# One block's scores and state sums moved behind the products of the block before, in the same four PSUM banks, and counted semaphore events put into TensorE's stream

## The chip, the cores and the metric

The kernel runs on one core of a Trainium2 chip. The metric is the device time of one execution in microseconds; the time before is the median of three runs. Profiles come from one more execution, which the hardware profiler records. TensorE is called PE, VectorE DVE, ScalarE ACT, GpSimd POOL and SyncE SP.

## The reference, cut to what matters

```python
# x: (4, 8, 768, 32), a: (4, 8, 768), B and C: (4, 8, 768, 16); chunks of 32 tokens
L = np.exp(cum[:, :, :, None] - cum[:, :, None, :]) * causal   # cum: running sum of log a
CB = np.einsum('bhin,bhjn->bhij', Cc, Bc)
y_intra = np.einsum('bhij,bhjd->bhid', CB * L, xc)
y_inter = np.einsum('bhin,bhnd->bhid', Cc, state) * np.exp(cum)[:, :, :, None]
Bx = np.einsum('bhjn,bhjd->bhjnd', Bc, xc) * np.exp(cum[:, :, -1:] - cum)[..., None, None]
state = np.exp(np.sum(la, axis=-1))[:, :, None, None] * state + np.sum(Bx, axis=2)
...
h = y @ w_in                                   # y as (3072, 256), w_in (256, 2048)
g = np.where(h > 0.0, h, np.exp(np.minimum(h, 0.0)) - 1.0)
out = g @ w_out                                # w_out (2048, 256)
```

A scan over tokens, with a state of 16 x 32 per head, gives y; a feed-forward layer with ELU follows.

## The kernel before, in words

The 3072 tokens are cut into twelve blocks of 256 tokens (8 heads each), three to a batch. The kernel scans in chunks of 64 tokens; u and v number a block's halves of 128 tokens and the halves of these. The blocks are numbered in the order of the work, so that neighbours belong to different batches. The whole order of the work is written out by hand, on every engine: an engine runs its instructions in the order in which the program gives them, and waits where an operand or a buffer isn't ready. PSUM has eight banks of 2 KB: seven rotate in one pool (p_a, tag "a"), one belongs to p_o. A tile takes the next bank of the rotation, and its first writer waits for the last reader of what was there before. The waits are put in by the framework, tile by tile.

The steps of block n, with the lines that the profile shows:

- Loads on SP's queue: `load_bc` (B and C, L140, in halves u), `load_x` (xr, L156), `spread_exp` (ec, the spread exponentials of the running sums, L404).
- `scaled` (L416 to 422): B times the decay factors, on the engine that is named (tile sc).
- `turn` (L436): four PE transposes (L442), of B into ps_tb and of C into ps_tc; ACT copies ps_tb to bt (L447); DVE makes ctm, C masked by heads (L450).
- `turn_exp` (L454): DVE multiplies ps_tc by ec into cts (L458). It is the last reader of ps_tc.
- `decay` (L553, L561): ACT takes exponentials of L, the decays of token pairs; POOL masks them (L566).
- `scores` (L572, L582): 32 small PE products from bt and ctm, into four banks ps_g, one for each pair of heads. `weigh` (L588, L591): DVE multiplies one bank by L into M.
- `sums` (L603, L612): 32 small products of sc and x into two banks ps_st. `states` (L619): DVE adds them to the running state (L629), POOL masks each new state into Sx (L634).
- `across` (L645, L660): products of Sx and cts into four banks ps_y. `inside` (L668, L678): products of M and x into the same banks; then six copies to yT (L695), on ACT for blocks 2 and 3.

The feed-forward layer of blocks 0 and 1, and the first half of it for blocks 2 and 3, uses plain float32 products: `l1` (L709, L716; eight products into a bank ps_h), `elu` (ACT L730 and L737, DVE L738) and `l2` (L893). For the second half of w_in's columns of blocks 2 and 3, and for all from block 4 on, two blocks together are done by `l1_words` (L824, L835): three passes over operands split into rounded words, six products for each m, joined by ACT and DVE; the words of y come from DVE, the tile y_both at L818. Behind each of these products for blocks 4 to 9 and m < 9 stands a sem_inc on a spare semaphore that nothing waits for (L838 to L840).

The stretch of the change is the loop over s (L1167 to L1209), which gives one l1 of blocks 0 and 1 for each s from 0 to 11 and lays the scan of block 2 between them: turn(2) at s=5, scores(2) at s=7, states(2) at s=8, across(2) and inside(2) at s=10. The loop over j that follows (L1233 to L1281; eight steps of one l1 of block 2 and one l2 of block 0) lays out block 3: scaled, turn and turn_exp at j=0, scores, sums and weigh at j=1, states at j=2, across and inside at j=3. Meanwhile w_out arrives in pieces that ACT, DVE and POOL round (L205 to L249). The loop j=8 to 15 (L1282 on) gives l1_words(2, j), an l2 of block 1 and the scan of blocks 4 and 5; the loop from L1368 on does the pairs of blocks from 4.

```python
                if 2 < n < 10 and m < 9:
                    for _ in range(1 + (n > 4 and k == 0)):
                        nc.tensor.sem_inc(spare, 1)
```

Of the kernel before, what the change touches and what calls it, by code (L numbers as in the profile page):

```python
# [17 lines left out]
P = 128  # L18
# [15 lines left out]
def kernel(  # L34
# [56 lines left out]
    def psum(shape, name):  # L91
        return p_a.tile(shape, F32, tag="a", name=name)
# [460 lines left out]
    def decay(n, q):  # L553

        decay_of(n, 2 * q)
        decay_of(n, 2 * q + 1)
# [12 lines left out]

    def scores(*ns, pool=p_a, tag="a"):  # L572

        gs = [psum([P, len(ns), 2, 2, Q], "ps_g") for _ in range(3)]
        gs.append(pool.tile([P, len(ns), 2, 2, Q], F32, tag=tag, name="ps_g"))
        for at, n in enumerate(ns):
            s = st[n]
            for u in range(2):
                for v in range(2):
                    for q in range(4):  # L580
                        rows, toks = slice(32 * q, 32 * q + 32), slice(Q * v, Q * v + Q)
                        nc.tensor.matmul(  # L582
                            out=gs[q][toks, at, u], lhsT=s["bt"][rows, u, toks],
                            rhs=s["ctm"][rows, u, :, toks], start=True, stop=True,
                            tile_position=(32 * q, Q * v), skip_group_check=True)
            s["g"], s["M"] = [g[:, at] for g in gs], []
# [13 lines left out]

    whole, most, last = slice(0, 4), slice(0, 3), slice(3, 4)

    def sums(*ns, pool=p_a, tag="a", parts=(None, None)):  # L603

        ps = [psum([P, len(ns), 2, 2 * D], "ps_st"),
              pool.tile([P, len(ns), 2, 2 * D], F32, tag=tag, name="ps_st")]
        for at, n in enumerate(ns):
            s = st[n]
            for u, v in chunks(n, parts[at] or whole):
                toks = slice(Q * v, Q * v + Q)  # L610
                for q in range(4):
                    nc.tensor.matmul(  # L612
                        out=ps[v][32 * q:32 * q + 32, at, u],
                        lhsT=s["sc"][toks, u, 2 * q:2 * q + 2].rearrange("p h n -> p (h n)"),
                        rhs=s["x"][toks, u, 2 * D * q:2 * D * (q + 1)], start=True, stop=True,
                        tile_position=(Q * v, 32 * q), skip_group_check=True)
            s["st"] = [p[:, at] for p in ps]
# [24 lines left out]

        return 2 * D * v if n else 0

    def across(*ns, pool=p_a, tag="a", halves=(0, 1)):  # L645


        y = [None, None]
        for t in halves:
            y[t] = [psum([P, len(ns), 2, Q], "ps_y"), (p_a if t else pool).tile(  # L650
                [P, len(ns), 2, Q], F32, tag="a" if t else tag, name="ps_y")]
        for u in (1, 0):
            for at, n in enumerate(ns):
                for v in range(2):
                    Sx = starts.get((n, u, v))
                    if Sx is None:
                        continue
                    for q in range(2 * halves[0], 2 * halves[-1] + 2):
                        rows, col = slice(32 * q, 32 * q + 32), (64 * q + shift(n, v)) % P
                        nc.tensor.matmul(  # L660
                            out=y[q // 2][v][col:col + 64, at, u],
                            lhsT=Sx[rows].rearrange("p k d -> p (k d)"),
                            rhs=st[n]["cts"][rows, u, Q * v:Q * v + Q],
                            start=(u == 1 and at == 0), stop=False,
                            tile_position=(32 * q, col), skip_group_check=True)
        return y

    def inside(y, *ns, t=None):  # L668
# [27 lines left out]
        if t:  # L696
            for n in ns:
                st.pop(n)


    g_of = {}

# [116 lines left out]
                out=both[:, k], in0=y1[:, k].bitcast(F32), scalar=1.0 - WORD,  # L819
                in1=y[:, k], op0=ALU.mult, op1=ALU.add)  # L820

    spare = tc.alloc_semaphore("spare")

    def l1_words(n, m, ahead=None, ahead_of_join=(), ahead_of_jobs=()):  # L824


        cols = slice(m % 2 * P, (m % 2 + 1) * P)
        w, w0 = k_words[m // 2]
        w1, both_w, w0 = w[:, 0, :, cols], w[:, 1, :, cols], w0[:, :, cols]
        y1, y0, both_y = y_words[n]  # L830
        high, both = psum([P, 2 * BLK], "ps_h"), psum([P, 2 * BLK], "ps_w")
        passes = [(high, w1, y1), (high, w0, y0), (both, both_w, both_y)]
        for ps, lhs, rhs in passes if n > 2 and m == 0 else passes[2:] + passes[:2]:
            for k in range(KC):
                nc.tensor.matmul(  # L835
                    out=ps, lhsT=lhs[:, k], rhs=rhs[:, k], start=k == 0 and lhs is not w0,
                    stop=k == KC - 1 and lhs is not w1)
                if 2 < n < 10 and m < 9:  # L838
                    for _ in range(1 + (n > 4 and k == 0)):
                        nc.tensor.sem_inc(spare, 1)  # L840
        if ahead and m == MC - 1:
            both_of_y(ahead, range(1) if n > 2 else range(KC))
            second_of_jobs()
            if n > 2:
                both_of_y(ahead, range(1, KC))
            third_of_jobs()
        e = ffn.tile([P, 2 * BLK], F32, tag="e", name="e", bufs=2)
        nc.scalar.activation(e, both, ACT.Copy, scale=WORD)  # L848
        first_of_jobs()
        if late:  # L850
            end_words()
        if ahead and m == MC - 2 and n > 2:
            high_of_y(ahead)
        for step in ahead_of_join:
            step()
        nc.vector.scalar_tensor_tensor(  # L856
            out=high, in0=high, scalar=WORD - 1.0, in1=e, op0=ALU.mult, op1=ALU.add)
        if ahead and m == MC - 2 and n > 2:
            low_of_y(ahead)
        for step in ahead_of_jobs:  # L860
            step()
        if not ahead or m != MC - 2:
            second_of_jobs()
        late.append((n, m, high, e))
# [302 lines left out]
    for s, (n, i) in enumerate((  # L1167
            (1, 0), (1, 1), (1, 2), (0, 4), (1, 3), (0, 5), (1, 4), (0, 6), (1, 5), (0, 7),
            (1, 6), (1, 7))):
        l1(n, i, by_half=s == 0)  # L1170
        if s < 8:
            decay_of(2, s)
        if s == 7:
            st[0] = kept
            scores(2)
            sums(2, 0, pool=p_o, tag="o", parts=(None, last))
            weigh(2, 0)
            weigh(2, 1)
        if s % 2 == 1 and todo < 11:
            w_take(todo, nc.vector)  # L1180
            w_give(todo)
            w_load(todo + 6)
            todo += 1
        if s in (1, 3):
            load_bc(3, us=(s // 2,))
        if s == 9:
            write_flat(0)
        if s == 4:
            scaled(2, nc.gpsimd)
        if s == 5:  # L1190
            turn(2)
            turn_exp(2)
        if s == 4:
            load_x(3)
            spread_exp(3)
        if s == 8:
            weigh(2, 2)
            weigh(2, 3)
            states(0, last)
            st.pop(0)  # L1200
            states(2)
        if s == 9:
            decay(3, 0)
            decay(3, 1)
        if s == 10:
            spread_cum(4)
            inside(across(2), 2)
        if len(lag) > 1:
            elu()  # L1209

# [22 lines left out]
    for j in range(2 * DIRECT):  # L1233
        n, i = 2 + j // DIRECT, j % DIRECT
        if j < 7:
            l2(0, j)
        piece = j in (0, 2, 3)
        if j == 0:
            elu()
        if piece:  # L1240
            w_take(todo, nc.vector)
        l1(n, i)
        if j == 7:
            l2(0, j)
        if j == 0:
            scaled(3, nc.gpsimd)
            turn(3)
            elu()
            turn_exp(3)
        if piece:  # L1250
            w_give(todo)
            todo += 1
        while lag:
            elu()
        if j == 0:
            decay(3, 2)
            decay(3, 3)
        if j == 1:
            scores(3)
            sums(3)  # L1260
            for q in range(4):
                weigh(3, q)
        if j == 2:
            states(3)
        if j == 3:
            inside(across(3), 3)
            w_take(14, nc.vector)
            w_give(14)
        if j == 4:
            words_of_y(2)  # L1270
            w_take(15, nc.vector)
            w_give(15)
        if j == 5:
            words_of_w(4)
            both_of_y(2)
            low_of_w(4)
        scan_ahead(j)
        if j == 6:
            words_of_w(5)
            low_of_w(5)  # L1280
            keep_words(4)  # L1281
# [205 lines left out]
```

## Time and profile before

| what | before |
|---|---|
| median of 3 runs (lowest to highest) | 338.31 us (337.97 to 338.34) |
| the profiled execution's own time | 339.09 us |
| its span in the profile | 337.4 us |
| granted TensorE clock, mean | 1.0 |
| PE's matmul instructions, busy | 3744, 329.9 us |
| DVE busy, share of the span | 286.6 us, 85% |
| ACT busy, share of the span | 259.6 us, 77% |
| l1 products of float32, L716 | 192, 44.8 us |
| l2 products of float32, L893 | 192, 45.5 us |

The span runs from the first to the last instruction in the profile; the execution's own time has a little more around it. Busy time counts the instructions that an engine executes; semaphore events on PE's sequencer aren't in it. Matmuls are pipelined, so the duration of a row of several is a little longer than the time until the next row starts; starts are what to compare. A timeline row gives the start, the duration, the engine, the line, the operation, output and inputs, and how many instructions it sums up; an idle time ahead of it and what ended it stand in brackets.

### The profile page before, as it was taken

What the parts mean: (1) busy time and instruction counts of PE and PEld (TensorE: products, weight loads), DVE (VectorE), ACT (ScalarE), POOL (GpSimd) and SP (SyncE); (2) the same over time, 40 slices, a digit from 0 to 9 for tenths busy, and PEclk for the clock granted to TensorE, in tenths of its full rate; (3) what the DMA queues carried; (4) which work ended last, traced back from release to release, by engine and by line L of the source; (5) the groups of instructions that cost most, each with busy time, mean ns of one, the idle gap of its engine ahead of it and who ended that gap; (6) DMA issues with size and microseconds to landing.
All of it is one profiled execution on the core that took longest, in us unless ns stands there. A gap on an engine that the chain in (4) does not pass through costs nothing.

```text
span 337.4 us, 9867 instructions
## 1 busy us (share of the span) xinstructions
PE 329.9 (98%) x3744; PEld 288.2 (85%) x3744; DVE 286.6 (85%) x511; ACT 259.6 (77%) x537; POOL 215.8 (64%) x242
## 2 busy tenths in 40 slices
PE   8799999999999999999999999999999999999995
PEld 6478888888888888888898888989989999999995
DVE  4898998889897889899989998989996978997942
ACT  5688989599858699858798867898867789897501
POOL 5453644547979396988588978488974355776000
PEclk9999999999999999999999999999999999999999
DMA  7888989655468379570769581868530863330001
GB/s 127 242 230 153 300 183 276 129 98 133 165 139 326 127 187 300 176 210 9 280 186 216 140 286 23 282 186 165 160 147 5 282 212 99 98 126 0 31 2 63
DMA packets 82957, 54.81 MB, mean 162 GB/s; under 512 B 59038, under 2 KB 68574, under 8 KB 82910
## 3 DMA queue, kind: packets, MB, share of 16 engines
q1 hardware_dynamic: 80734, 53.98, 56.9%
q8 instruction: 30, 0.49, 0.6%
q10 hardware_dynamic: 2176, 0.20, 0.5%
q14 instruction: 17, 0.14, 0.1%
HBM read 44.53 MB, written 9.63 MB: 161 GB/s over the span
## 4 chain that ended last, share of the span: by engine, by line
PE 91%; ACT 2%; DMA 2%; DVE 1%; POOL 1%; SPq 1%; issue 0%; DVEq 0%; POOLq 0%
PE ps_o L989 23%; PE ps_h L835 19%; PE ps_o L893 12%; PE ps_h L716 11%; PE ps_w L835 10%; PE ps_both L989 6%; PE ps_y L678 3%; PE ps_g L582 2%; PE ps_y L660 2%; DMA xr<-in_x_dram 2%; PE ps_st L612 1%; PE ps_high L989 1%; POOL w_in L249 1%; POOL g_words L907 0%; ACT e L848 0%
## 5 line engine op out<-in xcount | busy, mean ns | idle before, releaser
L907 POOL TENSOR_TENSOR g_words<-g_words,g_low 128x512 fp32r<-128x512 f32 x62 | 83.4, 1348 | 47.4 <-ACT e L868 17.2
L989 PE MATMUL ps_o<-o_words,g_words 128*128 128x256 f32 x448 | 83.3, 283 | 0.0
L989 PEld LDWEIGHTS ps_o<-o_words,g_words 128*128 128x128 f32 x448 | 73.0, 190 | 6.0 <-POOL g_words L907 1.1
L868 ACT ACTIVATE e<-ps_h 128x512 f32<-128x512 f32 x72 | 43.0, 597 | 36.3 <-DVE ps_h L856 36.3
L875 DVE SCALAR_TENSOR_TENSOR g<-e,ps_h 128x512 f32<-128x512 f32 x72 | 49.2, 684 | 19.8 <-ACT e L869 17.8
L989 PE MATMUL ps_o<-o_low,g_low 128*128 128x256 f32 x224 | 63.3, 283 | 0.0
L931 DVE SCALAR_TENSOR_TENSOR g_low<-g_words,g 128x512 fp32r<-128x512 f32 x72 | 63.1, 881 | 0.0
L856 DVE SCALAR_TENSOR_TENSOR ps_h<-ps_h,e 128x512 f32<-128x512 f32 x72 | 49.7, 691 | 2.7 <-ACT e L848 2.7
L835 PE MATMUL ps_w<-y_both,w_words 128*128 128x512 f32 x144 | 48.6, 419 | 0.0
L869 ACT ACTIVATE e<-e 128x512 f32<-128x512 f32 x72 | 45.5, 633 | 2.3
L716 PE MATMUL ps_h<-yT,w_in 128*128 128x256 f32 x192 | 44.8, 383 | 1.2 <-POOL w_in L249 1.1
L835 PE MATMUL ps_h<-y,w_words 128*128 128x512 f32 x144 | 45.4, 396 | 0.1
L893 PE MATMUL ps_o<-w_out,g 128*128 128x256 f32 x192 | 45.5, 380 | 0.0
L835 PE MATMUL ps_h<-y,w 128*128 128x512 f32 x144 | 44.8, 392 | 0.0
L848 ACT ACTIVATE e<-ps_w 128x512 f32<-128x512 f32 x72 | 42.0, 583 | 3.1 <-PE ps_w L835 3.1
L930 ACT ACTIVATE g_words<-g 128x512 fp32r<-128x512 f32 x72 | 43.6, 625 | 0.0
L989 PEld LDWEIGHTS ps_o<-o_low,g_low 128*128 128x128 f32 x224 | 42.7, 191 | 0.0
L716 PEld LDWEIGHTS ps_h<-yT,w_in 128*128 128x128 f32 x192 | 35.7, 190 | 7.1 <-POOL w_in L249 1.9
L893 PEld LDWEIGHTS ps_o<-w_out,g 128*128 128x128 f32 x192 | 36.1, 190 | 5.5
L835 PEld LDWEIGHTS ps_h<-y,w_words 128*128 128x128 f32 x144 | 26.6, 188 | 7.1 <-PE ps_w L835 1.0
L835 PEld LDWEIGHTS ps_h<-y,w 128*128 128x128 f32 x144 | 27.0, 188 | 6.4
L835 PEld LDWEIGHTS ps_w<-y_both,w_words 128*128 128x128 f32 x144 | 23.6, 191 | 1.8
(132 smaller groups left out, 549.4 us busy)
## 6 DMA issues: line engine op xcount, KB each, us to landing
w_words<-w_kept SPq DMA_DIRECT2D x28, 512.0 KB
w<-w_kept SPq DMA_DIRECT2D x28, 256.0 KB
L<-flat SPq DMA_DIRECT2D x20, 256.0 KB
w<-in_moe_w_out_dram SPq DMA_DIRECT2D x8, 512.0 KB
w_kept<-w_words SPq DMA_DIRECT2D x8, 512.0 KB
w<-in_moe_w_in_dram SPq DMA_DIRECT2D x7, 512.0 KB
xr<-in_x_dram SPq DMA_DIRECT2D x24, 128.0 KB
out_dram<-eo SPq DMA_DIRECT2D x18, 128.0 KB
```

The costliest lines, as they stand in the source:

```text
L716: nc.tensor.matmul(out=ps[:, j], lhsT=w_in[i][:, k, j * P:(j + 1) * P], rhs=yT[n // 2][:, k, n % 2].rearrange("p u i -> p (u i)"), start=( ...
L835: nc.tensor.matmul(out=ps, lhsT=lhs[:, k], rhs=rhs[:, k], start=k == 0 and lhs is not w0, stop=k == KC - 1 and lhs is not w1)
L848: nc.scalar.activation(e, both, ACT.Copy, scale=WORD)
L856: nc.vector.scalar_tensor_tensor(out=high, in0=high, scalar=WORD - 1.0, in1=e, op0=ALU.mult, op1=ALU.add)
L868: nc.scalar.activation(e, high, ACT.Relu, scale=-1.0)
L869: nc.scalar.activation(e, e, ACT.Exp, scale=-1.0)
L875: nc.vector.scalar_tensor_tensor(out=g_tile(n, m // 2)[:, m % 2].rearrange("p b i -> p (b i)"), in0=e, scalar=1.0, in1=h, op0=ALU.subtract ...
L893: nc.tensor.matmul(out=o_of[n][:, ts], lhsT=g_of[n // 2, j][:, m % 2, n % 2, ts * P:(ts + 1) * P], rhs=w_out[j][:, m % 2], start=(m == 0 a ...
L907: nc.gpsimd.tensor_tensor(out=out, in0=in0, in1=in1, op=ALU.subtract)
L930: yield nc.scalar.activation(words[:, 0], g, ACT.Copy, scale=NEAR / WORD)
L931: yield nc.vector.scalar_tensor_tensor(out=low, in0=words[:, 0].bitcast(F32), scalar=WORD, in1=g, op0=ALU.mult, op1=ALU.subtract)
L989: nc.tensor.matmul(out=ps, lhsT=lhs, rhs=rhs, start=lhs is both_g and first > 0 or lhs is g1 and first > 1, stop=last and lhs is not g1, s ...
```

## The change: what it does

Block 3's steps move from the loop over j into the loop over s, and four banks, each a tile ps_three of 512 columns, serve two blocks: columns 0 to 127 hold y of block 2 (across and inside), columns 128 to 255 of the first two banks the state sums of block 3, and columns 256 to 511 of all four the scores of block 3.

| step of block 3 | before | after |
|---|---|---|
| scaled (POOL) | j=0, behind l1 | s=8 |
| turn, turn_exp | j=0, behind l1 | s=9, ahead of decay(3, 0) and decay(3, 1) |
| scores, sums | j=1 | s=10, directly behind inside(2) in the program |
| states | j=2 | s=10, behind sums |
| weigh 0 and 1; 2 and 3 | j=1 | s=11; j=1 |

A function fill(count) gives that many sem_inc events on PE, and takes the place of the lines quoted above. Twelve stand behind l1 in each of s=0 to 5 (72, all new); in l1_words(2, m) six behind each product for m=8 and 9, five for m=11 and 12 (132, all new); in block 4 two behind each product for m < 9 instead of one (54 more). Blocks 6 and 8 keep theirs. In all PE's stream gets 258 more events (569 instead of 311); the number of products is the same. SP's list of transfers and its order are the same.

```diff
-    def scores(*ns, pool=p_a, tag="a"):
-
-        gs = [psum([P, len(ns), 2, 2, Q], "ps_g") for _ in range(3)]
-        gs.append(pool.tile([P, len(ns), 2, 2, Q], F32, tag=tag, name="ps_g"))
+    def scores(*ns, pool=p_a, tag="a", banks=None):
+
+        if banks:
+            gs = [b[:, 2 * P:4 * P].rearrange("p (n u k i) -> p n u k i", n=1, u=2, k=2) for b in banks]
+        else:
+            gs = [psum([P, len(ns), 2, 2, Q], "ps_g") for _ in range(3)]
+            gs.append(pool.tile([P, len(ns), 2, 2, Q], F32, tag=tag, name="ps_g"))
...
+        if banks:
+            ps = [b[:, P:2 * P].rearrange("p (n u e) -> p n u e", n=1, u=2) for b in banks[:2]]
...
+            y[t] = [b[:, 0:P].rearrange("p (n u i) -> p n u i", n=1, u=2)
+                    for b in banks[2 * t:2 * t + 2]] if banks else [psum([P, len(ns), 2, Q], "ps_y"), (p_a if t else pool).tile(
...
+    def fill(count):
+
+        for _ in range(count):
+            nc.tensor.sem_inc(spare, 1)
+
...
-                if 2 < n < 10 and m < 9:
-                    for _ in range(1 + (n > 4 and k == 0)):
-                        nc.tensor.sem_inc(spare, 1)
+                if n == 2:
+                    fill({8: 6, 9: 6, 11: 5, 12: 5}.get(m, 0))
+                elif n < 10 and m < 9:
+                    fill(2 if n == 4 or k == 0 else 1)
...
+        if s < 6:
+            fill(12)
+        if s == 8:
+            scaled(3, nc.gpsimd)
+        if s == 11:
+            weigh(3, 0)
+            weigh(3, 1)
         if s == 9:
+            turn(3)
+            turn_exp(3)
             decay(3, 0)
             decay(3, 1)
         if s == 10:
             spread_cum(4)
-            inside(across(2), 2)
+            banks = [psum([P, 4 * P], "ps_three") for _ in range(4)]
+            inside(across(2, banks=banks), 2)
+            scores(3, banks=banks)
+            sums(3, banks=banks)
+            states(3)
...
         if j == 0:
-            scaled(3, nc.gpsimd)
-            turn(3)
             elu()
-            turn_exp(3)
...
         if j == 1:
-            scores(3)
-            sums(3)
-            for q in range(4):
-                weigh(3, q)
-        if j == 2:
-            states(3)
+            weigh(3, 2)
+            weigh(3, 3)
```

More of the change, by code (lines that the diff above doesn't have):

```diff
@@ L601, with sums @@
     whole, most, last = slice(0, 4), slice(0, 3), slice(3, 4)
-    def sums(*ns, pool=p_a, tag="a", parts=(None, None)):
-        ps = [psum([P, len(ns), 2, 2 * D], "ps_st"),
-              pool.tile([P, len(ns), 2, 2 * D], F32, tag=tag, name="ps_st")]
+    def sums(*ns, pool=p_a, tag="a", parts=(None, None), banks=None):
+        if banks:
+            ps = [b[:, P:2 * P].rearrange("p (n u e) -> p n u e", n=1, u=2) for b in banks[:2]]
+        else:
+            ps = [psum([P, len(ns), 2, 2 * D], "ps_st"),
+                  pool.tile([P, len(ns), 2, 2 * D], F32, tag=tag, name="ps_st")]
         for at, n in enumerate(ns):
@@ L643, in shift, with across @@
         return 2 * D * v if n else 0
-    def across(*ns, pool=p_a, tag="a", halves=(0, 1)):
+    def across(*ns, pool=p_a, tag="a", halves=(0, 1), banks=None):
         y = [None, None]
         for t in halves:
-            y[t] = [psum([P, len(ns), 2, Q], "ps_y"), (p_a if t else pool).tile(
+            y[t] = [b[:, 0:P].rearrange("p (n u i) -> p n u i", n=1, u=2)
+                    for b in banks[2 * t:2 * t + 2]] if banks else [psum([P, len(ns), 2, Q], "ps_y"), (p_a if t else pool).tile(
                 [P, len(ns), 2, Q], F32, tag="a" if t else tag, name="ps_y")]
@@ L698, in inside @@
                 st.pop(n)
+    spare = tc.alloc_semaphore("spare")
+    def fill(count):
+        for _ in range(count):
+            nc.tensor.sem_inc(spare, 1)
     g_of = {}
@@ L820, in both_of_y @@
                 in1=y[:, k], op0=ALU.mult, op1=ALU.add)
-    spare = tc.alloc_semaphore("spare")
     def l1_words(n, m, ahead=None, ahead_of_join=(), ahead_of_jobs=()):
```

## The prediction

> **What bounds the kernel now.** Times are of the profiled execution: span 337.4 us, 1.7 around it, 339.09; the median of the three runs, 338.31, is 0.78 below, and I add the change to the median. First the page's engine list, the chain that ended last, and PE's waits.
>
> ```profile
> PE 329.9 (98%) x3744; PEld 288.2 (85%) x3744; DVE 286.6 (85%) x511; ACT 259.6 (77%) x537; POOL 215.8 (64%) x242
> ```
>
> ```profile
> PE 91%; ACT 2%; DMA 2%; DVE 1%; POOL 1%; SPq 1%; issue 0%; DVEq 0%; POOLq 0%
> ```
>
> ```profile
> PE ps_st L612 <- DMA xr<-in_x_dram: 1.2, 1, 1.2
> PE ps_h L716 <- POOL w_in L249: 1.1, 2, 1.0
> PE ps_idle L273 <- DVE idle L259: 1.1, 1, 1.1
> ```
>
> TensorE is the bound everywhere, and its largest named waits (total, times, longest) make 3.4 us. The change removes no product, so it can gain only idle time of PE; where it makes PE wait, the wait is paid in full. Next, PE around block 3 (start, duration):
>
> ```profile
> 43.00 5.45 PE L716 MATMUL ps_h<-yT,w_in 128*128 128x256 f32 x24
> 48.38 0.49 PE L660 MATMUL ps_y<-bct,Sx 32*64 32x64 f32 x32
> 48.79 0.88 PE L678 MATMUL ps_y<-M,xr 64*32 64x64 f32 x64
> ...
> 54.91 0.38 PE L442 MATMUL ps_tb<-ident,bc 128*128 128x128 f32 x2
> ...
> 58.90 0.69 PE L582 MATMUL ps_g<-ctm,bct 32*64 32x128 f32 x32
> 59.52 0.53 PE L612 MATMUL ps_st<-xr,sc 64*32 64x64 f32 x32
> ...
> 67.08 0.80 PE L660 MATMUL ps_y<-bct,Sx 32*64 32x64 f32 x32
> ```
>
> The first row is s=8, 9, 10 (8 products each, 0.216 apart, 1.73 a group), so s=9 ends near 46.5. The new place of turn(3) is there, 8.4 us ahead of 54.91; that of scores(3) is behind 48.79's row, at 49.6, 9.3 us ahead of 58.90.
>
> **1. The moved turn meets its loads.** These are the queue's issues on SP:
>
> ```profile
> 46.34 0.47 SPq L140 DMA_DIRECT2D bc<-in_B_dram  x1
> 46.85 0.58 SPq L140 DMA_DIRECT2D bc<-in_C_dram  x1
> 47.53 2.35 SPq L156 DMA_DIRECT2D xr<-in_x_dram  x2
> 49.98 0.67 SPq L404 DMA_DIRECT2D ec<-flat_exp  x1
> ```
>
> They are block 3's second halves of B and C, its x and its ec. In the trace's semaphore records they land at 50.2, 50.6, 52.6 and 52.9 (x in two), and 52.8. The order of SP's transfers is the same in both programs, and what holds these back is earlier transfers, not work that moves. So turn(3) cannot start at 46.5: the B transposes run at 50.2, the C ones end near 50.9, and s=10's products behind them end at 52.7 (before: 48.4). Behind turn(3) stand, in the programs' order, DVE's ctm and cts: cts reads ec, 52.84, plus 0.41 (L458's duration): 53.3. across(2) takes as its fourth bank the one that ps_tc(3) had, which cts reads: it begins at 53.4 instead of 48.4, inside(2) ends at 54.6 instead of 49.6. **5.0 us late.**
>
> **2. The shared banks wait for ACT.** The scores write other columns of the banks that inside(2) fills, but the program orders them behind the copies that empty y from each bank (L695). ACT's rows:
>
> ```profile
> 45.14 2.00 ACT L561 ACTIVATE L<-L,ncum 128x64 f32<-128x64 f32 x8
> 47.05 0.58 ACT L730 ACTIVATE e<-ps_h 128x512 f32<-128x512 f32 x1
> 47.66 0.63 ACT L737 ACTIVATE e<-e 128x512 f32<-128x512 f32 x1
> 49.31 1.66 ACT L695 COPY yT<-ps_y 128x128 f32<-128x128 f32 x6 [1.02 <-PE ps_y L678]
> ```
>
> New order: the copy of tb (50.6, 0.35), decay(3) (2.00), ELU (0.58+0.63), then the six copies. From 50.6 on these make 0.35+2.00+1.21 = 3.56, to 54.2; the first half of inside(2) is there by then, so the copies run from 54.3 to 55.95. The last bank is free at 56.0; scores(3), which use all four in turn, end 0.55 later, and sums(3) add 0.46: 57.0. Nine groups of 1.73 follow (one of s, eight of j), with 0.1 for the change back to large products: across(3) begins near 72.7 and, without a wait for Sx, lasts 0.42, to 73.1. Before, it ends at 67.81 (the start of the next row), so **steps 1 and 2 together cost +5.3**. The same from the parts: 5.0 late at the end of inside(2); 2.4 from there to the end of sums(3); less what the j loop no longer holds: turn(3) 0.44, scores and sums 1.08, the wait for Sx 0.3 (0.80 in the row at 67.08, 0.49 at 48.38), and some 0.3 of changes between large and small products. Bounds: from -0.5 (the gains at 67.08 and of the changes alone, loads and copies hidden) to +6.5 (if POOL's masks or Sx are late as well).
>
> What stands behind the new waits: on DVE, behind ctm and cts, the ELU end of s=9 and the conversions of w_out, in idle time (1.63 ahead of 52.28); on POOL, scaled(3) waits for B until 50.2 and takes 0.82, so that the w_out piece that ran at 50.13 is 0.9 late; its reader is a second product several rounds of 1.73 on, itself 5 us late. Those engines' work of the j loop comes later with PE, which leaves them no less room than now (ACT idles 2.89 before 63.74).
>
> **3. The added semaphore events.** fill() adds 258 instructions to PE's stream: 72 in s=0 to 5, 132 in l1_words(2, m), m=8, 9, 11, 12, and 54 in block 4. They aren't counted as busy, but PE's sequencer issues them in order with the products. Before has four behind each other at 168.13 to 168.59:
>
> ```profile
> L840 PEldq EVENT_SEMAPHORE  x4: 51/51/51, 168.1 to 168.6; - x4
> ```
>
> One lasts 51 ns, yet starts follow every 150 ns; of 54 pairs directly behind each other none is under 149. At 168.6 products wait for them: 300 ns to the next, instead of some 230. They are free only while the sequencer is ahead of the array (up to 3.9 us in this trace). Is it, at m=8?
>
> ```profile
> 82.36 0.81 PE L835 MATMUL ps_w<-y_both,w_words 128*128 128x512 f32 x2
> ...
> 83.93 1.89 PE L893 MATMUL ps_o<-w_out,g 128*128 128x256 f32 x8
> ```
>
> ```profile
> 79.36 2.20 DVE L818 SCALAR_TENSOR_TENSOR y_both<-y,yT 128x512 fp32r<-128x512 f32 x2
> ```
>
> The products read y_both, whose halves are ready at 80.5 and 81.6: the sequencer stood there, 1.8 us ahead. New: behind the second half five times six events, 30 x 0.15 = 4.5: l2's products are read at 86.1 instead of starting at 83.93: 2.2 late. m=9: 36 x 0.15 = 5.4 on an empty queue, l2(1,1) near 91.5 instead of 87.05: 4.5 in all. m=10 has none, and the queue fills again. m=11 waits for a bank that DVE's L591 frees, 0.5 ahead of its products (93.68): 30 events, 4.5, against 1.57 of products and 0.5: +2.4; m=12: 4.5 against a full round's 3.3, and the gaps: +1.5. **Sum +8.4.** The other events hide: in s<6 12 x 0.15 = 1.8 against a group's 1.73, at most 0.85 by s=6, which turn(3)'s wait takes; in block 4 12 events, 1.8, against 3.3 a round. Bounds: 0 (the sequencer 4 us ahead each time, and events cheaper when it waits) to 9.3. I take 8.4, as the rows at 82.36 and 79.36 fix the lead.
>
> [...] The trace shows no lead above 3.9, and at the two places here the lead is set by a wait, not by a full queue.
>
> **Sum:** 338.31 + 5.3 + 8.4 = 352.0; the profiled execution 339.09 + 13.7 = 352.8.
>
> **Rivals.** *A, the fills cost nothing* (the sequencer ahead, or later DVE work no longer late): 338.31+5.3 = 343.6. For it: before already has such events and PE stays at 98%; against: one or two behind a product there, six here. 0.12. *B, the loads come in time* (transfers ahead of them faster): only step 2's copies, some +1.8 with the fill in s<6, less 0.5, and the fills: 348 to 349. 0.05. *C, the clock drops.* At the start the granted clock rises at 6.37, with products since 1.10 (213 ns apart, then 109); at the end it falls 3.8 us after the last product (333.65 to 337.46); the idle stretch of 0.9 at 12.9 kept it. If turn(3)'s wait (3.7, or 2.8 when the fills of s<6 take 0.85 of it) and step 2's let it fall, the products run at twice the spacing for 2 to 4 us, and this is added: 354 to 357. 0.10. [...] *D, faster:* B and C of block 3 and ec land before 46.5 and 48, the copies aren't waited for, the events cost under 40 ns (6 x 0.04 = 0.24, a product's 0.22): 0.3+0.2 gained, and what PE idles else stays: 337.6. All three must hold; the issue rows at 46.34 speak against it. 0.04. *E, it does not do what it says:* the scores aren't directly behind inside(2), since the copies stand between; this is in the forecast.
>
> **How the numbers follow.** Forecast 0.67 (347 to 355), A 0.12, B 0.05, C 0.10, D 0.04, no change 0.02 (gains and waits cancel). A measurement tells 0.2%, 0.7 us. The likeliest gives 352.0. The range goes down to A, 343.2, and up into C, 356.5; outside are D, no change and half of C, with the tails. Faster 0.04, same 0.02, slower 0.94.
>
> **What would show it.** Step 1: L442's rows for block 3 at 50.2, PE idle some 3 us ahead of them, waiting for bc. Step 2: L582 behind the last L695 copy, not behind L678. Step 3: gaps of 0.7 to 0.9 between the L835 products of m=9, 11, 12, and l2(1,0) 2.2 late against the products before it. Wrong if L442 runs by 47.5, or if PE shows no gap between 82 and 105 (shifted).

## The result, and the profile after

The changed kernel takes 354.01 us (median of 6, 352.62 to 358.63) against 338.32 (median of 6, 337.97 to 339.00): 1.045 times the time, 95% interval 1.042 to 1.049. Measured once more beside the experiments it took 356.02 (354.12 to 358.45), 1.053 (1.051 to 1.056). The profiled execution took 352.62, its span 350.9, which is 13.5 more than the 337.4 of before. (Of the first six the longest, 358.63, is not in the ratio.)

The engine list and the chain of the page after:

```profile
PE 336.5 (96%) x3744; PEld 289.0 (82%) x3744; DVE 287.3 (82%) x511; ACT 260.5 (74%) x537; POOL 212.8 (61%) x242
...
PE 83%; ACT 6%; DVE 3%; issue 2%; SPq 2%; DMA 2%; POOL 0%; ACTq 0%; DVEq 0%; POOLq 0%
```

PE has the same products and more waits; 6% of the chain is now ACT and 2% "issue", time in which PE waited for nothing that the profile shows. PE's timeline around block 3 (start, duration, then what waited and the idle time ahead of it in brackets):

```profile
47.34 0.27 PE L442 MATMUL ps_tb<-ident,bc 128*128 128x128 f32 x1
49.21 0.33 PE L442 MATMUL ps_tb<-ident,bc 128*128 128x128 f32 x1 [1.59 <-DMA bc<-in_B_dram]
...
51.50 0.36 PE L667 MATMUL ps_three<-bct,Sx 32*64 32x64 f32 x12
52.37 0.45 PE L667 MATMUL ps_three<-bct,Sx 32*64 32x64 f32 x20 [0.51 <-DVE bct L458]
52.75 0.89 PE L685 MATMUL ps_three<-M,xr 64*32 64x64 f32 x64
53.58 2.08 PE L585 MATMUL ps_three<-ctm,bct 32*64 32x128 f32 x32
55.59 0.45 PE L618 MATMUL ps_three<-xr,sc 64*32 64x64 f32 x32
...
71.71 0.49 PE L667 MATMUL ps_y<-bct,Sx 32*64 32x64 f32 x32
72.13 0.88 PE L685 MATMUL ps_y<-M,xr 64*32 64x64 f32 x64
```

ACT's copies of y from the shared banks, and PE's row that follows block 3's across in the kernel before:

```profile
53.26 1.67 ACT L702 COPY yT<-ps_three 128x128 f32<-128x128 f32 x6 [0.26 <-PE ps_three L685]
```

```profile
67.81 0.88 PE L678 MATMUL ps_y<-M,xr 64*32 64x64 f32 x64
```

The half of B that was there is turned at once, the other waits 1.59. The scores take 2.08 instead of 0.69: each bank waits for its copy on ACT. Block 3's across ends at 72.13 instead of 67.81: the scan is 4.3 late there. The second place is l1_words(2, m), here m=8 and the start of l2's second group:

```profile
87.33 0.41 PE L848 MATMUL ps_h<-y,w_words 128*128 128x512 f32 x1
88.13 0.48 PE L848 MATMUL ps_h<-y,w_words 128*128 128x512 f32 x1 [0.39 <-issue]
89.08 0.46 PE L848 MATMUL ps_h<-y,w 128*128 128x512 f32 x1 [0.47 <-POOL L L566]
89.99 0.47 PE L848 MATMUL ps_h<-y,w 128*128 128x512 f32 x1 [0.44 <-POOL w L921]
90.93 3.65 PE L907 MATMUL ps_o<-w_out,g 128*128 128x256 f32 x8 [0.48 <-ACT o_words L930]
...
96.42 1.97 PE L907 MATMUL ps_o<-w_out,g 128*128 128x256 f32 x8 [0.46 <-issue]
```

The products stand 0.9 apart, six events of 0.15 (87.27 to 88.02 behind the second row, and so on). The engines in the brackets are only what happened to end last; the events are the wait. From 83.93 to 90.93 l2(1,0) is 7.0 late, of which 4.31 is brought along: 2.7 here. After m=12 the delay is 13.3, and from there it stays.

### The profile page after: what moved, and what is told of

It reads as the page before. It is cut to its first block, busy times and chain, and to the rows that moved or that the text cites. A ratio compares the mean times of both kernels' runs of the same rounds, so it can differ in the third digit from the quotient of the medians.

```text
span 350.9 us, 10125 instructions
## 1 busy us (share of the span) xinstructions
PE 336.5 (96%) x3744; PEld 289.0 (82%) x3744; DVE 287.3 (82%) x511; ACT 260.5 (74%) x537; POOL 212.8 (61%) x242
## 4 chain that ended last, share of the span: by engine, by line
PE 83%; ACT 6%; DVE 3%; issue 2%; SPq 2%; DMA 2%; POOL 0%; ACTq 0%; DVEq 0%; POOLq 0%
PE ps_o L1003 23%; PE ps_h L848 19%; PE ps_o L907 11%; PE ps_w L848 10%; PE ps_h L730 7%; PE ps_both L1003 5%; ACT L L561 2%; PE ps_y L685 2%; DMA w<-in_moe_w_in_dram 2%; PE ps_g L585 2%; PE ps_y L667 1%; PE ps_high L1003 1%; ACT e L744 1%; PE ps_st L618 1%; ACT yT L702 1%
## 5 line engine op out<-in xcount | busy, mean ns | idle before, releaser
L945 DVE SCALAR_TENSOR_TENSOR g_low<-g_words,g 128x512 fp32r<-128x512 f32 x72 | 64.9, 906 | 0.2 <-DMA L<-flat 0.2
L907 PE MATMUL ps_o<-w_out,g 128*128 128x256 f32 x192 | 47.4, 392 | 1.5 <-issue 1.0
L848 PE MATMUL ps_h<-y,w 128*128 128x512 f32 x144 | 45.6, 394 | 2.3 <-issue 1.4
L730 PE MATMUL ps_h<-yT,w_in 128*128 128x256 f32 x192 | 45.8, 385 | 1.7 <-POOL w_in L249 1.1
L907 PEld LDWEIGHTS ps_o<-w_out,g 128*128 128x128 f32 x192 | 37.0, 195 | 8.2 <-issue 1.9
```

The costliest lines, as they stand in the source:

```text
L730: nc.tensor.matmul(out=ps[:, j], lhsT=w_in[i][:, k, j * P:(j + 1) * P], rhs=yT[n // 2][:, k, n % 2].rearrange("p u i -> p (u i)"), start=( ...
L848: nc.tensor.matmul(out=ps, lhsT=lhs[:, k], rhs=rhs[:, k], start=k == 0 and lhs is not w0, stop=k == KC - 1 and lhs is not w1)
L907: nc.tensor.matmul(out=o_of[n][:, ts], lhsT=g_of[n // 2, j][:, m % 2, n % 2, ts * P:(ts + 1) * P], rhs=w_out[j][:, m % 2], start=(m == 0 a ...
L945: yield nc.vector.scalar_tensor_tensor(out=low, in0=words[:, 0].bitcast(F32), scalar=WORD, in1=g, op0=ALU.mult, op1=ALU.subtract)
```

## The experiments

Twelve runs. "Alone" in an edit means on the kernel before. Medians; ratios to the kernel before on the same chip.

| run | median us | ratio (95%) |
|---|---|---|
| e1_moves_alone | 350.05 | 1.036 (1.033 to 1.040) |
| e2_events_block2 | 355.43 | 1.051 (1.049 to 1.054) |
| e3_events_half | 345.15 | 1.020 (1.018 to 1.022) |
| e4_other_events | 352.39 | 1.041 (1.038 to 1.044) |
| e5_loads_early | 348.32 | 1.030 (1.026 to 1.034) |
| e8_events_hidden | 346.90 | 1.025 (1.021 to 1.030) |
| e9_hidden_early | 345.53 | 1.020 (1.018 to 1.023) |
| e10_page_of_events | 339.87 | 1.004 (1.002 to 1.006) |
| e11_nothing_late | 347.28 | see there |
| e12_spent_products | 343.21 | 1.015 (1.013 to 1.017) |
| e13_changed_again | 356.02 | 1.053 (1.051 to 1.056) |
| e14_border_moved | 343.22 | 1.013 (1.011 to 1.015) |

**The parts alone: e1 to e4.** My first theory was two causes that add: 4.3 for the moves, 9.0 for the events of m=8 to 12, nothing for the other events.

```diff
# e1: the changed kernel without its events; those of before are kept
...
-        if s < 6:
-            fill(12)
...
# e2, on the kernel before, behind each product of l1_words
+                if n == 2:
+                    for _ in range({8: 6, 9: 6, 11: 5, 12: 5}.get(m, 0)):
+                        nc.tensor.sem_inc(spare, 1)
# e3: the same with 3 for each of the four m
# e4, on the kernel before: 12 in each s < 6; in block 4 two behind each product
```

> The changed kernel with the events of before: the moved steps and the shared banks alone. The theory of two separate causes reads the price of the moves from the changed kernel's trace: block 3's across ends at 72.13 us instead of 67.81, so +4.3, and 338.3 + 4.3 = 342.6 (341.8 to 343.6). Rival one, the events are free and the moves cost everything: 352 to 354. Rival two, the moves cost nothing, since what is late at 72 is given back later in the j loop: 338 to 339.

> The kernel before, with only the 132 events of l1_words(2, m), m = 8, 9, 11, 12. The theory reads +9.0 from the changed kernel's trace (the delay grows from 4.31 to 13.36 us between the first product of m=8 and block 4's across): 338.3 + 9.0 = 347.3 (346 to 349). Rival, an event costs nothing and the gaps there are a late effect of the moves: 338.3.

> The kernel before, with 3 events behind each of the six products of m = 8, 9, 11, 12 (72 in all) instead of 6 and 5. The theory is a rate: an event takes the sequencer 0.15 us, so a round has 18 x 0.15 = 2.7 us of events against 3.1 to 3.3 us of products, and the sequencer stays ahead: 338.3 (338 to 339). Rival, each event holds up the array by a fixed time, 9.0 / 132 = 0.069 us: 72 x 0.069 = 4.9, 343.2.

> The kernel before, with only the other 126 new events: 12 in each of s = 0 to 5, and 2 instead of 1 behind each product of block 4. The rate theory: 1.8 us of events against 1.73 us of products in s < 6, late by at most 0.85 us at s=6 if no lead was there, and hidden in block 4 (1.8 against 3.3): 338.3 to 339.2. Rival, a fixed price of 0.069 us each: 126 x 0.069 = 8.7, 347.

All four miss. The three disjoint parts of the change cost 11.7 (e1), 17.0 (e2) and 14.0 (e4), 42.7 in all, and together they cost 15.7. No sum of prices does that. PE's waits show the missing piece; the first line is of e2, the second of e3, the third of e4 (waited for: total, times, longest):

```profile
PE ps_y L678 <- issue: 6.7, 4, 2.2
```

```profile
PE ps_y L678 <- issue: 3.7, 1, 3.7
```

```profile
PE ps_y L678 <- issue: 8.5, 4, 3.5
```

The kernel before has no such wait. It falls inside the run of small products of inside(), in e3 here:

```profile
102.01 1.34 PE L678 MATMUL ps_y<-M,xr 64*32 64x64 f32 x110
107.10 0.53 PE L678 MATMUL ps_y<-M,xr 64*32 64x64 f32 x18 [3.75 <-issue]
```

If PE's instructions (weight loads, products, events) are counted in the order of the program, the product that waits is number 3010 in e2, in e3 and in e4 alike, though 132, 72 and 72 added events stand ahead of it: the 81st product of inside() in e2, the 111th in e3 and e4. The other waits of e2 and e4 are at 4290, 5570 and 6850, with 132 and some 126 added events ahead. These are 5 x 256 apart. The instruction queue of the trace moves 16 KB a packet (0.49 MB in 30 packets on the page before), and one packet belongs to each 256 instructions: PE's weight loads, products and events are 7799 before and 8057 after, 30.5 and 31.5 times 256, and the pages have 30 and 31 packets. In e3 the border before, number 2754, is passed at about 101.7; the packet starts at 104.8 and takes 1.0; PE, which waits at number 3010, goes on at 107.1, 1.3 behind the packet's end. So I read this as code that comes late: here the block behind border 3010 is moved only when border 2754 has been passed, and both borders lie in one run of quick instructions (across and inside).

With small products some 13 ns apart (64 in 0.84 in the row at 48.79 of before) the late packet isn't hidden: e3 waits 3.75 us.

The rate theory itself held. From the first product of m=8 to l2 behind m=12 it is 16.02 before (82.36 to 98.38), 17.05 with e3's 72 events (82.30 to 99.35) and 24.73 with e2's 132 (81.59 to 106.32): 1.0 and 8.7, where a fixed price of 0.069 would give 4.9 and 9.1. e4's 72 events in s < 6 cost 1.4 (from the first l1 of s=0 to turn(2) 11.82 instead of 10.46), where a fixed price would give 5.0. The clock drops at the waits too: in e3 it is at half from 107.2 to 110.6. e1 has the wait for code in the merged burst, between the sums, at number 1730 (its waits: total, times, longest), and its clock drops to half at 54.5, ahead of that wait, for 6.8 us:

```profile
PE ps_tb L442 <- DMA bc<-in_B_dram: 2.9, 1, 2.9
PE ps_three L618 <- issue: 1.3, 1, 1.3
```

**Is it the borders? e10 and e8.** The change adds 258 events, one block and 2.

```diff
# e8: the changed kernel, the events of m = 8 to 12 moved; e10: e4 with the same
         if j < 7:
             l2(0, j)
+            fill(8)
...
         l1(n, i)
+        fill(8 + (j % 2 == 0))
...
```

> The kernel before with 258 added events and no move: the 126 that alone made it 352.4, and 132 in the loop over j, 8 or 9 behind each group of eight products. Block theory: 258 is a whole block and 2, so every border from m=8 on stands where it stood, and the events are hidden: 338.4 (338 to 339.5), though it holds all the events that cost 14 us and 132 more. Rival, events have a price each: 352 or more.

> The changed kernel, with the 132 events of l1_words(2, m) moved into the loop over j, 8 or 9 behind each group of eight products (1.2 to 1.35 us of events against 1.73 of products). PE's instructions from m=13 on keep their numbers, so the borders of the code blocks stay where the changed kernel has them. Rate and block theory together: the 9.0 us of the events in m = 8, 9, 11, 12 go and nothing comes for them: 354.0 - 9.0 = 345 (343 to 346). Rival, an event has a fixed price wherever it stands: 354. Rival, the place of the borders among the products of m=8 to 12 matters as well: 346 to 350.

e10 holds every event of e4 (352.39) and 132 more, and takes 339.87: 12.5 less, and no wait "issue" is left among PE's waits. 1.4 is left, and its timeline shows that much in s=0 to 5, among the events (11.82 from the first l1 to turn(2) instead of 10.46). PE before, then in e10:

```profile
27.25 10.63 PE L716 MATMUL ps_h<-yT,w_in 128*128 128x256 f32 x48
37.71 0.38 PE L442 MATMUL ps_tb<-ident,bc 128*128 128x128 f32 x2
```

```profile
26.88 1.99 PE L718 MATMUL ps_h<-yT,w_in 128*128 128x256 f32 x8
29.35 9.51 PE L718 MATMUL ps_h<-yT,w_in 128*128 128x256 f32 x40 [0.47 <-PE ps_h L718]
38.70 0.38 PE L442 MATMUL ps_tb<-ident,bc 128*128 128x128 f32 x2
```

The block theory is shown: the same events cost 14 or 1.4, by where the borders fall. e8 gives 346.9, 7.1 less than the changed kernel's 354.0 instead of 9.0, 0.9 above the range (and 9.1 less than the 356.0 of e13, so that much of the miss is within what the changed kernel's own time varies). In its profile l2(1,0) is no later than the products ahead of it, so the rate's 9 us are gone; 1.0 came as a wait for code at number 3010, and the clock was at half from 55.8 to 62.6, where the changed kernel's profile has it full. The time lies in the range of the last rival, but the profile shows no wait among the products of m=8 to 12.

**The loads: e5 and e9.**

```diff
     spread_cum(3)
+    load_bc(3)
+    load_x(3)
+    spread_exp(3)
     w_load(10)
...
-        if s in (1, 3):
-            load_bc(3, us=(s // 2,))
...
-            load_x(3)
-            spread_exp(3)
```

> The moves alone (events as before), with block 3's B, C, x and ec asked for ahead of two pieces of w_out, so that they land some 5 us sooner. The block theory: PE's instructions come in blocks of 256, the next block but one is asked for when a block's border is passed, and borders less than some 5 us apart make PE wait. In the moves alone the borders at instructions 1474 and 1730 both lie in the merged burst. Without the wait for loads the burst lasts about 4 us (products 2.5, copies 1.4), so a wait for code of 1 to 2.5 us stays, with the copies' 1.4, less 0.5 of gains: 338.4 + 2 to 3.5 = 340.4 to 342 (350.05 with the late loads). Rival, the loads are the moves' whole price: 338 to 339. Rival, the loads play no part: 348 to 350.

> The kernel before this one in the list (events hidden in the loop over j), with block 3's loads asked for earlier as well. Theory: the 4.0 us of waiting for the loads go as well, and what stays is the wait of the scores for ACT's copies, 1.4, less some 0.5: 338.4 + 0.9 = 339.3 (338.5 to 340.5). Rival, the merged burst costs no more once its data are there, and gains: 337.8. Rival, the loads that are now later (w_out's pieces) become the wait: 341 to 345.

Both miss: 1.7 and 1.4 less than without, not 9 and 7.6. PE no longer waits for bc, but it now waits longer for cts. PE and then DVE in e9 (B and C are there at 45.0, ec at 47.4):

```profile
49.52 0.36 PE L667 MATMUL ps_three<-bct,Sx 32*64 32x64 f32 x12
52.15 0.45 PE L667 MATMUL ps_three<-bct,Sx 32*64 32x64 f32 x20 [2.27 <-DVE bct L458]
...
53.36 2.54 PE L585 MATMUL ps_three<-ctm,bct 32*64 32x128 f32 x32
...
56.44 3.78 PE L730 MATMUL ps_h<-yT,w_in 128*128 128x256 f32 x8
```

```profile
48.94 0.74 DVE L218 TENSOR_SCALAR w_out<-w 128x512 f32<-128x512 uint32 x1
...
50.38 0.69 DVE L239 SCALAR_TENSOR_TENSOR mag<-mag 128x512 uint32<-128x512 uint32 x1
50.99 0.68 DVE L450 TENSOR_TENSOR ctm<-ps_tc,hmask 128x512 f32<-128x512 f32 x1
51.59 0.41 DVE L458 TENSOR_TENSOR bct<-ps_tc,ec 128x256 f32<-128x256 f32 x1
```

DVE is never idle there: the piece of w_out that s=9 converts stands ahead of ctm in its order. In the changed kernel cts starts at 51.80, when ec lands (51.78) and DVE is just done with ctm: two causes at one time, and taking one away gives little. Its DVE:

```profile
51.20 0.68 DVE L450 TENSOR_TENSOR ctm<-ps_tc,hmask 128x512 f32<-128x512 f32 x1
51.80 0.42 DVE L458 TENSOR_TENSOR bct<-ps_tc,ec 128x256 f32<-128x256 f32 x1
```

The last row of PE in e9 shows the second price: a group of l1 in 3.78 instead of 1.89, at half clock, from 53.5 to 60.4.

**The clock: e12.** On e9, six more products go where PE waits for DVE; nobody reads them.

```diff
+            spent = p_o.tile([P, 2, BLK], F32, tag="o", name="ps_spent")
+            for _ in range(6):
+                nc.tensor.matmul(
+                    out=spent[:, 0], lhsT=w_in[0][:, 0, 0:P],
+                    rhs=yT[0][:, 0, 1].rearrange("p u i -> p (u i)"), start=True, stop=True)
             banks = [psum([P, 4 * P], "ps_three") for _ in range(4)]
...
-        fill(8 + (j % 2 == 0))
+        fill(8 + (j % 2 == 0) - 3 * (j > 3) * (j < 8) - 3 * (j < 4))
```

> The kernel with hidden events and early loads (345.5), with six more products of 128x256 ahead of block 2's across, into a spare bank that nobody reads, 12 x 0.216 = 2.6 us, where PE waits 2.3 for DVE, and 24 events fewer, so that the borders stay. Clock theory: the gate halves the clock by the work of windows of 3.41 us; with the wait filled, the 6.8 us at half clock go, in which l1 and l2 took 2.0 us more and the scores 0.5: 345.5 + 0.3 - 2.3 = 343.5 (342.8 to 344.3). Rival, the small products of the burst alone halve the clock, waits or not: 345.8 (345.3 to 346.5).

343.21 as expected, with a mean clock of 0.997 to 1.0 in its four executions: work added, 2.3 us won. The wait filled took the half clock with it; the 3.41 of the theory is the length of the half clock in the changed kernel's profile (from 90.99), and that the work of such a window sets the clock isn't shown. Across now starts at 51.93 without a wait, and the group behind the burst takes 1.99:

```profile
49.25 2.75 PE L1228 MATMUL ps_spent<-yT,w_in 128*128 128x256 f32 x12
51.93 0.49 PE L667 MATMUL ps_three<-bct,Sx 32*64 32x64 f32 x32
...
55.58 1.99 PE L730 MATMUL ps_h<-yT,w_in 128*128 128x256 f32 x8
```

**Nothing late, and the border moved: e11 and e14.**

```diff
# e11, on e9: turn(3), turn_exp(3) from s=9 to s=8; weigh(3, 0), (3, 1) from s=11 to j=1
             sums(3, banks=banks)
+            decay(3, 0)
+            decay(3, 1)
             states(3)
...
# e14, on e11
-        if s < 6:
+        if s < 11:
             fill(12)
...
-            fill(8)
+            fill(4)
...
-        fill(8 + (j % 2 == 0))
+        fill(5)
```

> The changed kernel with its late pieces put right: events hidden in the loop over j, block 3's loads asked for early, turn(3) and turn_exp(3) at s=8 (on DVE ahead of the w_out piece of s=9 instead of behind it), decay(3, 0) and (3, 1) behind the copies on ACT, weigh(3, 0) and (3, 1) at j=1. The theory names four prices of the move (loads, DVE's queue, ACT's queue, half clock that follows from them), and leaves the wait for the six copies, some 0.9, and 0.7 of the events in s < 6, less 0.5: 338.4 + 1.1 = 339.5 (338.4 to 340.5). Rival, the shared banks themselves are the price: 342 to 344.

> The kernel with the four late pieces put right (341.8 to 348.3), with 60 of its hidden events moved from the loop over j to s = 6 to 10. Nothing else differs. The border at instruction 1730 then stands 174 instructions into the merged burst instead of 234, and the one ahead of it in the l1 of s=8 instead of that of s=9, so that the block of code behind 1730 has some 7 us to come instead of some 5. Block theory: the wait of 3.3 us inside the scores goes, and the half clock that follows it: 339.5 to 341 in nearly all executions, with a clock near 1.0. Rival, the burst itself (4.5 us without a large product) brings the half clock, and so the spread: 344 to 348.

e11 ranges from 341.82 to 348.27, so that the table gives no ratio. The median misses the range by 6.8, and even the fastest execution, at full clock, by 1.3. Its profile (347.74) has across at 50.02 without a wait, and then code that comes late inside the scores, number 1730:

```profile
51.27 1.87 PE L585 MATMUL ps_three<-ctm,bct 32*64 32x128 f32 x20
56.45 0.72 PE L585 MATMUL ps_three<-ctm,bct 32*64 32x128 f32 x12 [3.30 <-issue]
```

The border ahead, 1474, was passed near 47.5; its packet started only at 54.0, with the 16 DMA engines busy with data all that time (share 0.87 to 1.09 in the windows from 44 to 56). The clock is at half from 55.6, within that wait, to 62.4. In e14 the border 1474 is further ahead, the wait for code and the half clock are gone, and the executions lie within 0.9 us (342.94 to 343.86). The median misses the range by 2.2: across begins at 52.16 instead of e11's 50.02. Of these 2.1, 1.5 come at once by the rate of the 60 events that I moved, where twelve of them stand behind the burst of s=7 (eleven follow each other from 43.81 to 45.32, and DVE in the bracket only ended last):

```profile
45.42 1.97 PE L730 MATMUL ps_h<-yT,w_in 128*128 128x256 f32 x8 [1.46 <-DVE mag L232]
...
53.51 2.08 PE L585 MATMUL ps_three<-ctm,bct 32*64 32x128 f32 x32
```

What stays is the copies' wait: L585 takes 2.08 again. So e14's 4.6 above before are accounted for, as an estimate from these rows: 1.4 for the events of s < 6, 2.1 for the 60 moved, 1.4 for the copies' wait, less some 0.3. No run shows the merged burst without any of these prices, and none beats the kernel before.

**The spread: e13.**

> The changed kernel once more, for its spread (352.6 to 358.6 against 338.0 to 339.0 of before). Clock theory: a window of 3.41 us at half clock falls on the merged burst or on m = 8 to 12 in some executions, more often the longer the time: 353 to 356, with a mean clock of 0.985 to 1.0. Rival, the loads' time of arrival makes the spread: equal clocks.

The median, 356.02, is at the upper end of the forecast, but the clock isn't what spreads these six: all have a mean clock of 0.989 or 0.990 (two drops, at 92.0 and 109.1 in the profile), as the rival says, and lie 4.3 apart (354.12 to 358.45). In the first six the longest times come with the lowest clocks (356.26 at 0.988, 358.63 at 0.985). In this profile ec landed at 53.6 instead of 51.8, so that across waits 1.5 instead of 0.5; that the loads make the spread of the executions without a profile isn't shown.

## Why the prediction was right, point by point

The time forecast was 352.0 and the measured one 354.0, in the range, and slower as forecast. The profiled span, 350.9, was 351.1 by the forecast. The steps:

- *Step 1, the moved turn meets its loads.* Right as a wait, 1.0 too late: B's second half landed at 49.2 instead of 50.2, and across's waiting products started at 52.4 instead of 53.4. Its reason for cts was incomplete: I put the conversions of w_out behind ctm and cts, and they stand ahead (e9), so that DVE alone would hold cts as long as ec does.
- *Step 2, the shared banks wait for ACT.* Right: 2.39 from the end of inside (53.58) to the end of the sums (55.97), 2.4 by the forecast. What holds the scores is the length of the six copies (1.67), not what stood ahead of them on ACT: ACT was idle for 0.26 before the first copy, where I had it busy to 54.2, and in e9 it was idle for 1.94. Steps 1 and 2 together: +4.3 instead of +5.3.
- *Step 3, the events' rate.* Right in mechanism and near in size: 2.7, 5.1 after m=9, 2.1 for m=11, 1.8 for m=12, 9.0 in all against 8.4. e3 and e8 show the mechanism: with enough products beside them the events cost little (1.0 for e3's 72). A sequencer far enough ahead to hide them, the forecast's bound of 0, would have left +5.3 in all; the 9.0 speak against it. The events of s < 6 cost 1.34 (11.80 from the first l1 to turn(2), instead of 10.46), not at most 0.85; turn(3)'s wait took it, as forecast: B is waited for 2.90 without these events (e1) and 1.59 with them.
- *What step 3 left out: the number of the events.* I counted them as a price and saw no effect of their number. It moves the borders of the code. Rival A, "the fills cost nothing", 343.6, asked the wrong question: without them the moves cost 350.05 (e1). The scores begin at the same time in e1's profile as in the changed kernel's (53.60 and 53.58), and the second large group behind them 3.9 later (61.66 instead of 57.80): 1.3 of that is the wait for code, and the clock is at half from 54.5 on. It was luck that the forecast came out near: 258 events are a whole block and 2 and leave the borders of all that follows where they were (e10), while other numbers, 132 alone or 126 alone, bring 17 and 14 us, of which my step holds at most 9. In the burst the borders stand 6 us apart (49.2 and 55.2) with the 72 events and 5.5, with a wait of 1.3 in it, without them; no run changes this alone.
- *Rival C, the clock.* Given 0.10, with its place at turn(3). It takes part in nearly every execution (five of the first six have a mean clock under 1). In the profiled one it falls at 91.0, among the events of m=8, and is hidden there: the 36 events of m=9 follow each other some 0.15 apart from 90.97 to 96.31 without a break, and the products of m=9 would have waited for them anyway. That the median lies 2.0 above the forecast and 1.4 above the profiled execution may come from these drops and from later loads (e13); how much is whose in executions without a profile isn't shown.
- *Rival E, the scores aren't directly behind inside.* So it is: the copies stand between.

## What to carry to other kernels

In these traces semaphore events on PE's sequencer follow each other 0.15 us apart, and products beside them hide that (72 cost 1.0 in e3, 132 in the same place 8.7 in e2); and their number, counted with PE's other instructions, decides where the borders of 256 fall (the same events cost 14.0 in e4 and 1.4 in e10). So an edit that adds or takes PE instructions is compared twice, once as it is and once with the count made up to a whole block, and a wait "issue" within a run of small products (3.75 in e3, 3.30 in e11) is read as code that comes late. A step moved ahead is checked against every queue at its new place: here the loads and DVE's queue held cts to the same time, ACT was ready only 0.26 ahead of need, and curing the loads showed DVE's queue at once (e5, e9).

## What the runs showed of the hardware that I had not expected

- **Half clock without a long idle time.** The clock's record for the changed kernel is at half from 90.99 for 3.413 us. In the 3.41 us ahead of that PE had no idle time above 0.5, but only 1.62 of work (windows: length, then busy time and instructions of PE, PEld, DVE, ACT, POOL, granted clock, DMA share, GB/s):

```profile
87.58:90.99 3.41, 1.62 (x5) 0.65 (x4) 3.41 (x7) 3.15 (x9) 3.26 (x5) 1.00 0.66 247
90.99:94.40 3.41, 3.41 (x9) 2.72 (x9) 1.55 (x3) 1.23 (x2) 3.26 (x5) 0.50 0.50 175
```

  Other profiles have such stretches too: 3.4 us in e3 (107.2 to 110.6), 6.8 in e1, e8, e9 and e11, and some 10.2 in e5 (from about 53.6), so one, two or three times 3.41. The changed kernel's stands 85.333 us behind the clock's rise at 5.65, 25 times 3.4133. The stretch ahead of it was worked to 47%. Busy time alone doesn't decide it: the changed kernel's stretch 46.61 to 50.03, busy for 1.83 with large products, was followed by full clock, and e1's from 51.06 to 54.47, busy for 2.63 but mostly with small products, by half. What sets the clock stays open.
- **Late code beside full DMA engines.** From the border's passing to PE going on it took some 5.4 us in e3 and some 9 in e11; the packet itself takes 1.0, and PE goes on 1.3 to 1.5 behind its end. The rest is the time until the packet starts, 3.1 and 6.5, with the DMA engines full in both (0.93 to 1.06, and 0.87 to 1.09). Where a border falls into small products and the DMA engines are nearly idle (share 0.00 to 0.09 from the border to the packet), the packet starts 0.6 to 0.8 behind it (0.61 at 100.20, 0.84 at 221.41 and 0.79 at 272.03 in the changed kernel, 0.81 at 208.33 before); with full engines it is 2.4 at 101.29 before (share 0.99), but only 0.8 at 59.11 (1.22), so a full share alone doesn't say how late.
